# Row and column maxima of an attention and soft-MoE kernel: from a TensorE product to VectorE copies between partition quadrants

## The chip, the cores and the metric

The kernel runs on one core of a Trainium2 chip. The metric is device time in microseconds (us) of one launch. A core has engines that run side by side, each with its own queue of instructions: TensorE (PE in the profile, with PEld for its weight loads), VectorE (DVE), ScalarE (ACT), GpSimd (POOL) and SyncE (SP, which here only issues DMAs). Data lie in SBUF, with 128 partitions, and in the smaller PSUM, into which TensorE writes. A quadrant is a set of 32 neighbouring partitions. VectorE works along the columns of each partition; it can transpose blocks of 32 x 32 but its reductions don't cross the quadrants.

## The reference

First an attention in which keys and values are the same: 16 neighbouring pixels of kv are averaged and multiplied by w_sr. Then a soft mixture of experts over all tokens, whose dispatch is a softmax over the tokens (down each column) and whose combination is a softmax over the slots (along each row).

```python
kv_pool = kv.reshape(B, H // r, r, W // r, r, C).mean(axis=(2, 4))
k = v = kv_pool.reshape(B, -1, C) @ w_sr
s = scale * (q @ k.transpose(0, 2, 1))
s = s - s.max(-1, keepdims=True)
a = np.exp(s)
a /= a.sum(-1, keepdims=True) + 1e-09
x = (a @ v).reshape(B * N, C)

logits = x @ phi
d = np.exp(logits - logits.max(0, keepdims=True))
d /= d.sum(0, keepdims=True) + 1e-09
slot_input = (d.T @ x).reshape(E, S_per_e, D)
for e in range(E):
    slot_out[e] = np.maximum(slot_input[e] @ w1[e], 0.0) @ w2[e]
c = np.exp(logits - logits.max(1, keepdims=True))
c /= c.sum(1, keepdims=True) + 1e-09
out = c @ slot_out
```

Here B = 4 batches of 12288 queries with C = 128 channels meet 768 keys each; there are 8 experts with 4 slots each, so 32 columns in the logits.

## The kernel before

The 49152 queries are cut into 96 blocks of 512. For each block, `qk` makes the scores with the keys on the partitions: six tiles of 128 keys x 512 queries, two to a PSUM tile (`s0`, `s1`, `s2`), each from three products because queries and keys are split in a high and a low part. The softmax needs for each query the maximum over all 768 keys, which lie on partitions and in tiles. That is the row-maximum chain:

- `rowmax1` (L480, three times a block): VectorE transposes blocks of 32 x 32 on the fly and takes the maximum over the 32 keys of each quadrant. What is left has 96 columns: six tiles of keys, 16 groups of 32 queries.
- `rowmax2` (L490, L492): a maximum over the six tiles, then a product with `quad`, which puts each quadrant's 16 numbers in columns of its own, with zeros elsewhere.
- `rowmax_pe` (L500): a TensorE product with `sel`, a matrix of ones where two partitions have the same number within their quadrant. It brings the four quadrants' numbers, side by side, to every partition.
- `rowmax3` (L505): the maximum over the four.
- `rowmax4` (L510): VectorE transposes back and spreads, so that each partition has the maximum of every query (`mb`).

Then `sub` (L518, four pieces) subtracts it from the scores, which frees the three PSUM tiles for the next block. `exp_hi` (L525) and `exp_t` (L529) take the exponential on ScalarE, `plo` (L534) makes the low part on GpSimd, and `av_hi` and `av_lo` (L551, L552, L559) multiply with the values on TensorE, some two blocks later. `av_evac` (L569) brings the result to SBUF.

Four blocks make a group (`group_ops`) for the first half of the mixture: a softmax over the tokens with a running column maximum. `g2` (L628, L630) takes the maximum over the group's tokens in each quadrant. `g2q` spreads it with `quad` on ScalarE, `g3m` (L639) multiplies it with `sel` on TensorE, and `g3` (L644 to L651) takes the maximum over the quadrants, transposes it and updates the running maximum `MRUN`. `g4` to `g7a` use it. After the last block comes a tail with the experts and the combination.

Two PSUM banks, the ring `m`, serve all products but the scores: attention outputs, sums of the groups, keys and values of the next batch, and the products with `sel`. The product of the row maxima uses the top columns of a bank and may lie beside an attention output.

The order of instructions on PE, DVE, ACT and POOL isn't left to a scheduler: `Plan` simulates the engines with a cost for each operation and a due time made of `PER`, the planned time of a block, and writes each engine's queue in the order that results. An operation marked `hot`, as the row-maximum chain is, is kept free of others that would delay it (`HOLD`). `raw` is the wait that the plan reckons between two dependent operations of one engine.

## Time and profile before

| | |
|---|---|
| median of 3 runs | 1114.38 us (1112.85 to 1114.99) |
| profiled execution: its time, its span | 1114.22 us, 1112.4 us |
| mean granted clock of TensorE | 0.975 |
| busy over the span: PE, DVE, ACT, POOL | 1046.7, 984.9, 822.7, 866.2 us |
| first and last row-maximum product (L492 to L500) | 30.1 and 1003.3 us |

The span runs from the first to the last instruction; some 2 us of the time lie around it. Up to about 25 us the first keys are loaded and pooled, from there to about 1010 us the blocks follow one another, and the rest is the tail, with the output's DMAs.

A row of a group names line, engine, operation, output and inputs, shapes and count; then busy time in us and the mean length of one in ns; then the engine's idle time before these instructions and what ended it. A row of the timeline has start, length, engine and line. Shares of several engines don't add up to anything, as they run side by side.

### The profile page before, as it was taken

How to read it: one execution, taken by the hardware profiler on the slowest of the kernel's cores; microseconds unless marked ns; L12 is line 12 of the kernel's file. 1: busy time of each engine (PE TensorE's matmuls, PEld its weight loads, DVE VectorE, ACT ScalarE, POOL GpSimd, SP SyncE). 2: the span in 40 equal slices, each digit the busy share in tenths (PEclk: the TensorE clock that was granted, in tenths of full speed). 3: DMA queues.
4: the chain of work that ended last, by engine and by line, in shares of the span. 5: the costliest groups of instructions: out<-in, count | busy, mean ns of one | idle time of the engine just before them, and what ended most of it. 6: DMA issues, size and time to landing. Idle time of an engine off the chain costs nothing.

```text
span 1112.4 us, 24632 instructions
## 1 busy us (share of the span) xinstructions
PE 1046.7 (94%) x10198; PEld 897.3 (81%) x10198; DVE 984.9 (89%) x1492; ACT 822.7 (74%) x1006; POOL 866.2 (78%) x480
## 2 busy tenths in 40 slices
PE   3699999999999999999999999999999999997876
PEld 2588888888888888888888888888888888886343
DVE  7899889889889989899899988989989988987895
ACT  1677778778778778878877788688788777875563
POOL 0579897788899888789889889779889889773340
PEclk9799999999999999999999999999999999999885
DMA  9315421111125310120136210120110110113398
GB/s 342 117 22 132 96 44 39 39 58 39 39 54 124 91 42 22 39 70 27 39 83 123 71 53 1 39 96 2 39 39 1 39 39 2 39 39 115 141 407 360
DMA packets 17407, 89.15 MB, mean 80 GB/s; under 512 B 1680, under 2 KB 3984, under 8 KB 11152
## 3 DMA queue, kind: packets, MB, share of 16 engines
q1 hardware_dynamic: 13408, 69.47, 16.8%
q0 software_dynamic: 3312, 17.70, 8.4%
q8 instruction: 81, 1.33, 0.5%
q10 hardware_dynamic: 576, 0.41, 0.1%
q14 instruction: 30, 0.25, 0.1%
HBM read 58.87 MB, written 25.17 MB: 76 GB/s over the span
## 4 chain that ended last, share of the span: by engine, by line
PE 67%; DVE 27%; issue 2%; ACT 2%; POOL 1%; DMA 1%; SPq 0%; DVEq 0%; ACTq 0%; POOLq 0%
PE m L551 11%; PE m L552 10%; PE m L559 10%; PE s L473 9%; PE s L475 9%; PE s L474 9%; DVE t L518 8%; DVE r L480 8%; PE m L500 3%; PE m L690 2%; DVE mb L510 2%; PE po L1120 2%; DVE o L1129 2%; DVE cm L628 1%; DVE pool L311 1%
## 5 line engine op out<-in xcount | busy, mean ns | idle before, releaser
L534 POOL TENSOR_TENSOR plo<-t,phi 128x1536 f16<-128x1536 f32 x190 | 595.8, 3143 | 125.1 <-ACT t L529 123.8
L525 ACT ACTIVATE phi<-t,lnk 128x1536 f16<-128x1536 f32 x192 | 301.6, 1571 | 133.5 <-DVE t L518 132.9
L480 DVE TRANSPOSE_TENSOR_REDUCE r<-s 128x32 f32<-128x1024 f32 x288 | 349.8, 1236 | 27.1 <-PE s L475 21.1
L551 PE MATMUL m<-vhi,phi 128*128 128x161 f16 x2280 | 354.5, 234 | 2.5 <-DVE m L505 1.3
L552 PE MATMUL m<-vlo,phi 128*128 128x160 f16 x2280 | 353.5, 233 | 0.0
L518 DVE TENSOR_TENSOR t<-s,mb 128x1024 f32<-128x1024 f32 (+1 forms) x384 | 342.9, 949 | 8.8 <-DVE mb L510 0.9
L529 ACT ACTIVATE t<-t,lnk 128x1536 f32<-128x1536 f32 x192 | 299.8, 1568 | 2.3
L551 PEld LDWEIGHTS <-phi 128*128 128x128 f16 x2304 | 227.0, 99 | 22.9 <-issue 22.8
L473 PE MATMUL s<-qhi,khi 128*128 128x512 f32 x576 | 238.1, 413 | 6.5 <-DVE t L518 6.1
L552 PEld LDWEIGHTS <-phi 128*128 128x128 f16 x2304 | 225.5, 98 | 5.2 <-issue 3.3
L475 PE MATMUL s<-qhi,klo 128*128 128x512 f32 x576 | 227.2, 394 | 0.0
L474 PE MATMUL s<-qlo,khi 128*128 128x512 f32 x576 | 226.6, 393 | 0.0
L559 PE MATMUL m<-vhi,plo 128*128 128x161 f16 x2280 | 221.9, 233 | 0.3 <-POOL plo L534 0.3
L559 PEld LDWEIGHTS <-plo 128*128 128x128 f16 x2304 | 174.8, 100 | 1.3 <-issue 0.6
L463 POOL TENSOR_TENSOR qlo<-q,qhi 128x512 fp32r<-128x512 f32 x96 | 125.7, 1310 | 26.9 <-ACT qhi L459 26.9
L569 ACT ACTIVATE xl<-m 128x322 f32<-128x322 f32 x189 | 81.0, 428 | 76.1 <-PE m L559 75.7
L473 PEld LDWEIGHTS s<-qhi,khi 128*128 128x128 f32 x576 | 109.7, 190 | 29.9 <-issue 3.6
L475 PEld LDWEIGHTS s<-qhi,klo 128*128 128x128 f32 x576 | 109.2, 190 | 24.6 <-DVE klo L353 0.5
L474 PEld LDWEIGHTS s<-qlo,khi 128*128 128x128 f32 x576 | 109.8, 191 | 20.3 <-issue 0.7
L510 DVE STREAM_TRANSPOSE mb<-m 128x512 f32<-128x512 f32 x96 | 68.3, 711 | 3.3
L459 ACT ACTIVATE qhi<-q 128x512 fp32r<-128x512 f32 x96 | 59.2, 617 | 2.4 <-issue 1.0
L505 DVE TENSOR_REDUCE m<-m 128x16 f32<-128x64 f32 x96 | 21.5, 224 | 40.5 <-PE m L500 40.5
(140 smaller groups left out, 854.1 us busy)
## 6 DMA issues: line engine op xcount, KB each, us to landing
q<-qT SPq DMA_DIRECT2D x23, 1024.0 KB, 4.8
outT<-o SPq DMA_DIRECT2D x21, 1024.0 KB, 5.2
kva<-kvT POOLq DMA_DIRECT2D x9, 1536.0 KB, 11.4
kva<-kvT SPq DMA_DIRECT2D x3, 1536.0 KB, 10.5
kv<-kv SPq DMA_DIRECT2D x8, 512.0 KB, 5.7
w<-w SPq DMA_DIRECT2D x2, 1536.0 KB, 6.4
w<-w SPq DMA_DIRECT2D x4, 768.0 KB, 4.6
outT<-o SPq DMA_DIRECT2D x6, 512.0 KB, 4.3
```

What stands on the lines that cost most here:

```text
L463: nc.gpsimd.tensor_tensor(out=lo, in0=q_src(i), in1=hi.bitcast(F32), op=ALU.subtract)
L473: nc.tensor.matmul(s, khi[:, ks], hi, start=True, stop=False)
L474: nc.tensor.matmul(s, khi[:, ks], lo, start=False, stop=False)
L475: nc.tensor.matmul(s, klo[:, ks], hi, start=False, stop=True)
L480: nc.vector.tensor_reduce(out=MX[i][:, 2 * u : 2 * u + 2, :].rearrange("p t b -> p (t b)"), in_=S[i, u].rearrange("p t (b j) -> p (t b) j" ...
L518: nc.vector.tensor_tensor(out=TT_[i, h][:, o : o + n, :], in0=S[i, t // 2][:, u : u + n, :], in1=MX[i].unsqueeze(1).broadcast_to([P, n, BQ ...
L525: nc.scalar.activation(hi, TT_[i, h], AF.Exp, bias=lnk, scale=SCALE)
L529: nc.scalar.activation(t, t, AF.Exp, bias=lnk, scale=SCALE)
L534: eng.tensor_tensor(out=lo, in0=TT_.pop((i, h)), in1=PP[i, h], op=ALU.subtract)
L551: nc.tensor.matmul(px, p, vhi[:, t, :], start=(t == 0), stop=False)
L552: nc.tensor.matmul(px[:, 1:], p, vlo[:, t, :], start=False, stop=False)
L559: nc.tensor.matmul(px, PP[i, t // TH][1][:, t % TH, ks], vhi[:, t, :], start=False, stop=(t == NT - 1))
```

## The change

Row maxima and column maxima no longer go through TensorE. In `rowmax2` the maximum over the tiles is written to the first 16 columns of `rq`, in SBUF; three VectorE copies bring the numbers of quadrants 1, 2 and 3 to columns of their own in quadrant 0. In `rowmax3` four VectorE reductions, all reading quadrant 0, write the maximum over the quadrants to one quadrant each. `rowmax_pe` is gone. The groups do the same in `g2` and `g3`, with one column in place of 16; `g2q` and `g3m` are gone, and the running maximum is now a reduction over a pair of neighbouring columns' blocks, the old maximum and the group's.

The PSUM banks are no longer used for any of this. The plan's numbers change with it: a block is planned at 9.5 us, the new operations have costs of their own, and some costs of TensorE's products are lower, so that the order of the queues can differ from before in other places too. The pair that holds the high and the low part of the exponentials is made earlier; what is computed there is the same.

```diff
-    PER = 9.8
+    PER = 9.5
...
     def rowmax2(i):
-        top = banks[plan.bank][:, 512 - (NQD + 1) * NBK :]
-        pq = PQ[i] = top[:, NBK:]
-        r1 = top[:, :NBK]
-        nc.vector.tensor_reduce(out=r1, in_=MX[i].rearrange("p t b -> p b t"), axis=X, op=ALU.max)
         rq = sp.tile([P, NQD, NBK], F32, tag="rq", name=f"rq_{i}")
-        nc.vector.tensor_tensor(
-            out=rq, in0=r1.unsqueeze(1).broadcast_to([P, NQD, NBK]),
-            in1=quad.unsqueeze(2).broadcast_to([P, NQD, NBK]), op=ALU.mult,
-        )
+        nc.vector.tensor_reduce(out=rq[:, 0, :], in_=MX[i].rearrange("p t b -> p b t"), axis=X, op=ALU.max)
+        for k in range(1, NQD):
+            nc.vector.tensor_copy(rq[:Q32, k, :], rq[k * Q32 : (k + 1) * Q32, 0, :])
         MX[i] = rq
-
-    def rowmax_pe(i):
-        pqv = PQ.pop(i)
-        nc.tensor.matmul(pqv, sel, MX[i].rearrange("p k b -> p (k b)"), start=True, stop=True)
-        MX[i] = pqv
 
     def rowmax3(i):
         m1 = sp.tile([P, NBK], F32, tag="m1", name=f"m1_{i}")
-        nc.vector.tensor_reduce(out=m1, in_=MX[i].rearrange("p (k b) -> p b k", k=NQD), axis=X, op=ALU.max)
+        for k in range(NQD):
+            nc.vector.tensor_reduce(
+                out=m1[k * Q32 : (k + 1) * Q32, :], in_=MX[i][:Q32].rearrange("p k b -> p b k"), axis=X, op=ALU.max
+            )
         MX[i] = m1
...
-        d["cmt"] = sm2(g, "cmt", [P, 1])
-        nc.vector.tensor_reduce(out=d["cmt"], in_=cm, axis=X, op=ALU.max)
-
-    def g2q(g):
-        d = G[g]
         d["cq"] = sm2(g, "cq", [P, NQD])
-        scale(g, d["cq"], quad, d["cmt"])
-
-    def g3m(g):
-        pc = G[g]["pc"] = mt([P, 512], f"pc_{g}")
-        nc.tensor.matmul(pc[:, :NQD], sel, G[g]["cq"], start=True, stop=True)
+        nc.vector.tensor_reduce(out=d["cq"][:, :1], in_=cm, axis=X, op=ALU.max)
 
     def g3(g):
         d = G[g]
+        cq = d["cq"]
+        for k in range(1, NQD):
+            nc.vector.tensor_copy(cq[:Q32, k : k + 1], cq[k * Q32 : (k + 1) * Q32, :1])
         c1 = sm2(g, "c1", [P, 1])
-        nc.vector.tensor_reduce(out=c1, in_=d["pc"][:, :NQD], axis=X, op=ALU.max)
-        d["gm"] = d["pc"][:, NS : 2 * NS]
-        nc.vector.transpose(out=d["gm"], in_=c1.broadcast_to([P, NS]))
-        MRUN[g] = gp.tile([P, NS], F32, tag="mrun", name=f"mrun_{g}", bufs=3)
+        for k in range(NQD):
+            nc.vector.tensor_reduce(out=c1[k * Q32 : (k + 1) * Q32, :], in_=cq[:Q32], axis=X, op=ALU.max)
+        MR[g + 1] = gp.tile([P, 2, NS], F32, tag="mrun", name=f"mrun_{g}", bufs=3)
+        new = MRUN[g] = MR[g + 1][:, 0, :]
         if g == 0:
-            nc.vector.tensor_copy(MRUN[g], d["gm"])
+            nc.vector.transpose(out=new, in_=c1.broadcast_to([P, NS]))
         else:
-            nc.vector.tensor_tensor(out=MRUN[g], in0=MRUN[g - 1], in1=d["gm"], op=ALU.max)
+            nc.vector.transpose(out=MR[g][:, 1, :], in_=c1.broadcast_to([P, NS]))
+            nc.vector.tensor_reduce(out=new, in_=MR[g].rearrange("p k n -> p n k"), axis=X, op=ALU.max)
...
-        go("2q", small, sm_(1), [o["2"]], g2q)
-        mc, md = ("m", ("pc", g)), ("m", ("pd", g))
-        go("3m", "PE", 0.25, [o["2q"]], g3m, acq=[mc])
-        go("3", "DVE", 0.45, [o["3m"]] + ([ops["g3", g - 1]] if g else []), g3, use=[mc])
+        go("3", "DVE", 1.3, [o["2"]] + ([ops["g3", g - 1]] if g else []), g3)
...
-                "PE", 3 * 0.2315, 0.17, T0 - QKP + 0.65 * t, [ops["ql", i]] + kd[: 1 if t < KSPLIT // P else 2] + ([ops["qk", i, t - 1]] if t else [ops["qk", i - 1, NT - 1]] if i else []),
+                "PE", 3 * 0.2275, 0.17, T0 - QKP + 0.65 * t, [ops["ql", i]] + kd[: 1 if t < KSPLIT // P else 2] + ([ops["qk", i, t - 1]] if t else [ops["qk", i - 1, NT - 1]] if i else []),
...
-        r2 = op("DVE", 0.36, 0.08, T0 + 2, [ops["r", i, NU - 1]], lambda i=i: rowmax2(i), acq=[("m", ("pq", i)), ("rq", i)], use=[("r6", i)], hot=True, raw=0.14)
-        pe = op("PE", 0.27, 0.3, T0 - 10, [r2], lambda i=i: rowmax_pe(i), use=[("m", ("pq", i)), ("rq", i)], hot=True)
-        r3 = op("DVE", 0.12, 0.08, T0 - 10, [pe], lambda i=i: rowmax3(i), acq=[("m1", i)], use=[("m", ("pq", i))], hot=True)
-        r4 = op("DVE", dve(BQ) - 0.03, 0.08, T0 - 10, [r3], lambda i=i: rowmax4(i), acq=[("mb", i)], use=[("m1", i)], hot=True, raw=0.14)
+        r2 = op("DVE", 0.46, 0.08, T0 + 2, [ops["r", i, NU - 1]], lambda i=i: rowmax2(i), acq=[("rq", i)], use=[("r6", i)], hot=True, raw=0.1)
+        r3 = op("DVE", 0.4, 0.08, T0 - 10, [r2], lambda i=i: rowmax3(i), acq=[("m1", i)], use=[("rq", i)], hot=True, raw=0.18)
+        r4 = op("DVE", dve(BQ) + 0.03, 0.08, T0 - 10, [r3], lambda i=i: rowmax4(i), acq=[("mb", i)], use=[("m1", i)], hot=True, raw=0.18)
```

The costs of the AV products in the plan go from 0.0705 to 0.0695 (`av_hi`) and from 0.072 to 0.070 (`av_lo`) for each matmul.

## The prediction

> **What bounds the kernel now.** I read the busy times first, then the steady stretch from 100 to 1000 us, then what VectorE waits for there.

> ```profile
> 100.00:1000.00 900.00, 889.53 (x8898) 783.85 (x8897) 815.05 (x1202) 706.72 (x841) 776.89 (x415) 1.00 0.18 49
> ```

> The columns are length, then busy time of PE, weight loads, DVE, ACT and POOL, the granted clock, the DMA share and GB/s. TensorE is busy 889.5 of 900 us at full clock, so it sets the pace; VectorE follows with 815.1. The groups of VectorE in the same stretch show how near it is:

> ```profile
> L480 DVE TRANSPOSE_TENSOR_REDUCE r<-s 128x32 f32<-128x1024 f32 x264 | 320.1, 1235 | 24.2 <-PE s L475 18.7
> L518 DVE TENSOR_TENSOR t<-s,mb 128x1024 f32<-128x1024 f32 x176 | 214.4, 1218 | 8.1 <-DVE mb L510 0.9
> L510 DVE STREAM_TRANSPOSE mb<-m 128x512 f32<-128x512 f32 x88 | 62.6, 711 | 3.0
> L490 DVE TENSOR_REDUCE m<-r 128x16 f32<-128x96 f32 x88 | 28.8, 328 | 5.3
> L492 DVE TENSOR_TENSOR rq<-m,quad 128x64 f32<-128x64 f32 x88 | 19.7, 224 | 3.0
> L505 DVE TENSOR_REDUCE m<-m 128x16 f32<-128x64 f32 x88 | 19.7, 223 | 35.8 <-PE m L500 35.8
> L696 DVE TENSOR_TENSOR acc<-acc,m 128x129 f32<-128x129 f32 x22 | 6.2, 282 | 2.2 <-ACT acc L585 2.2
> ```

> The stretch holds 88 blocks (x88), so one block takes 900 / 88 = 10.23 us. Of VectorE's 900 - 815 = 85 us idle, 35.8 is the wait for the matmul of the row maxima, 18.7 the wait for scores and 2.2 a wait for ScalarE. The other 28.2 us are short gaps before dependent instructions, which I count as not to be filled. One block of VectorE is thus 815 / 88 + 28.2 / 88 = 9.26 + 0.32 = 9.58 us of work and 0.65 us of waits. Both engines stand close to the limit, and the change takes work from one and gives work to the other.

> **What goes.**

> ```profile
> L500 PE MATMUL m<-rq,sel 128*128 128x64 f32 x176 | 36.7, 290 | 8.1 <-DVE rq L492 7.5
> L639 PE MATMUL m<-cq,sel 128*128 128x4 f32 x46 | 6.7, 216 | 0.0
> ```

> TensorE loses 36.7 + 6.7 us of work and 8.1 us of idle time in the stretch. Its floor falls from 889.5 / 88 = 10.11 to (889.5 - 43.4) / 88 = 9.61 us a block. Were TensorE still the bound, 0.5 us x 96 blocks = 48 us would go (1066 us). That is the far low end. What is late next is VectorE.

> ScalarE loses a scaling per group, worth nothing here, as it is busy 706.7 of 900. The two PSUM banks lose two tenants, the product of the row maxima and that of the column maxima. No row shows a large wait for a bank, so I give that nothing. No DMA moves, and SP's and POOL's queues issue the same instructions as before. The new waits are all of VectorE on itself, in the row-maximum chain; what stands behind them is the transpose L510 and the four subtractions L518, which ScalarE's exponentials and the next scores wait for, so nothing covers them.

> VectorE's fixed part is what stays when the chain from L490 to L510 is cut out. From busy time and gaps it loses L490, L492, L505 and the gap before L492: 815.1 + 28.2 - 28.8 - 19.7 - 19.7 - 3.0 = 772.1 us, or 8.77 us a block. The gaps before L490 and L510 stay in this number.

> **What the new chain costs.** It is a reduction of 96 columns, three copies of 32 x 16, and four reductions of 32 x 64 to 32 x 16, one for each quadrant. The trace has no instruction on 32 partitions, so I take the same shapes on 128.

> ```profile
> 1027.48 0.26 DVE L1025 COPY sm<-m 128x16 f32<-128x16 f32 x2
> L1025 DVE COPY sm<-m 128x16 f32<-128x16 f32 x2 | 0.3, 170 | 0.1
> 439.61 0.32 DVE L490 TENSOR_REDUCE m<-r 128x16 f32<-128x96 f32 x1
> 439.97 0.22 DVE L492 TENSOR_TENSOR rq<-m,quad 128x64 f32<-128x64 f32 x1
> 440.78 0.22 DVE L505 TENSOR_REDUCE m<-m 128x16 f32<-128x64 f32 x1 [0.50 <-PE m L500]
> 441.04 0.71 DVE L510 STREAM_TRANSPOSE mb<-m 128x512 f32<-128x512 f32 x1
> ```

> Two independent copies of 16 columns take 0.17 us each and 0.26 us together: the second starts 0.09 us after the first, an overlap of 0.08 us. A dependent instruction starts 0.03 to 0.04 us after the end of the one before (440.78 + 0.22 to 441.04). So:

> - reduction, as L490: 0.33, and 0.03 to the copies
> - three copies, pitch 0.09: 2 x 0.09 + 0.17 = 0.35, and 0.03
> - four reductions as L505, pitch 0.22 - 0.08 = 0.14: 3 x 0.14 + 0.22 = 0.64

> The sum is 1.38 us. Before, the same stretch was 1.43 us from start to start (439.61 to 441.04), 0.50 of it a wait. Seen so, the change shortens the chain's latency a little, but it turns a wait into work, and the wait could hold other work.

> The durations are uncertain both ways. L505 reads PSUM in strides; the new reductions read SBUF in strides, as L238 below did: 128 columns in 0.36 us, against 0.28 for L244, which reads the same columns in order.

> ```profile
> 9.27 0.36 DVE L238 TENSOR_REDUCE sel<-ident 128x32 f32<-128x128 f32 x1
> 9.55 0.28 DVE L244 TENSOR_REDUCE quad<-ident 128x4 f32<-128x128 f32 x1
> 9.74 0.22 DVE L240 COPY sel<-sel 128x128 f32<-128x128 f32 x1
> ```

> That 0.08 us on 128 columns would be 0.04 to 0.05 on 64, in each of four: up to 0.2 more. Downward, a reduction that writes SBUF could be 0.08 shorter than L490, which writes PSUM, and copies could follow each other at 0.06: together 0.16 less. I take 1.38, by the rows of the same shapes.

> **The groups.** Before the running maximum there were L644, L646 and L651; now there are three copies of one column, four reductions of four columns, the same transpose, and a reduction of pairs.

> ```profile
> 1018.35 0.16 DVE L644 TENSOR_REDUCE c<-m 128x1 f32<-128x4 f32 x1 [0.81 <-PE m L639]
> 1018.55 0.23 DVE L646 STREAM_TRANSPOSE m<-c 128x32 f32<-128x32 f32 x1
> 1018.81 0.19 DVE L651 TENSOR_TENSOR mrun<-mrun,m 128x32 f32<-128x32 f32 x1
> ```

> Added: copies 0.35 + 0.03, reductions 3 x 0.08 + 0.16 + 0.03 = 0.43, pairs 0.22 + 0.03. That is 1.06 us. Gone: 0.16 + 0.19 + 0.03 = 0.38. So 0.68 us for each group of four blocks, 0.17 a block; bounds 0.1 and 0.3.

> **The sum.** VectorE's block is 8.77 + 1.38 + 0.17 = 10.32 us, against 10.23 now. TensorE's 9.61 is out of the way. The difference is 0.09 us x 96 blocks = 9 us. The profiled execution took 1114.2 us (span 1112.4), 0.2 under the median of the three runs, so the forecast is **1123 us**. The own range of this case: with the 0.16 taken off, 10.16 us and 1107; with 0.2 for the strides and 0.2 for waits on scores that stay (18.7 / 88), 10.73 us and 1162.

> **Rivals.**

> *Faster: the small operations cost less than their lookalikes.* The chain and the group together pay as long as 8.77 + chain + 0.17 stays under 10.23, so the point from which it turns is a chain of 1.29 us, only 0.09 under my sum. With 0.25 for the first reduction, copies 0.06 apart (0.27 together), and reductions 0.09 apart with 0.20 for the last (0.47), it is 1.05 with its two gaps, the block 9.99, and the gain 0.24 x 96 = 23 us: 1091. For it speaks that TensorE then leaves more than 0.3 us of slack; against it that no row has such a pitch for 64 columns. Chance 0.31.

> *Slower: the small operations don't overlap.* Each copy reads another quadrant, and each reduction writes another; in the trace before all neighbours start on the same partitions, so the overlap of 0.08 us is not shown for these. Without it, five neighbours in the chain (two copies, three reductions) cost 0.08 to 0.11 more each, 0.40 to 0.55, and five in a group a quarter of that per block. The block is 10.82 to 11.01 us, and the time 1171 to 1189, about 1180. Chance 0.22. [...]

> *Slower by much: the copies wait for GpSimd.* L240 copied 128 columns within SBUF in 0.22 us, where L244 needed 0.28 to reduce as many, so such a copy seems to use more of the memory's paths. And the trace shows VectorE stopped by GpSimd:

> ```profile
> 7.94 1.22 DVE L311 TENSOR_TENSOR pool<-pool,kv 128x1024 f32<-128x1024 f32 x1 [0.39 <-DMA kv<-kv]
> L311 DVE TENSOR_TENSOR pool<-pool,kv x12: 681/956/2165, 7.9 to 23.4; 128x1024 f32<-128x1024 f32 x6, 128x512 f32<-128x512 f32 x6
> 10.67 1.54 POOL L463 TENSOR_TENSOR qlo<-q,qhi 128x512 fp32r<-128x512 f32 x1 [9.14 <-ACT qhi L459]
> L534 POOL TENSOR_TENSOR plo<-t,phi 128x1536 f16<-128x1536 f32 x176 | 551.2, 3139 | 105.0 <-ACT t L529 103.7 <-DVE cm L628 0.8
> L463 POOL TENSOR_TENSOR qlo<-q,qhi 128x512 fp32r<-128x512 f32 x87 | 113.5, 1305 | 0.0
> ```

> One addition of two SBUF tiles took 2.17 us in place of 1.22; the only GpSimd work of that stretch, 10.67 to 12.21, lies beside it. If a copy also waits for GpSimd's running instruction, the mean rest of one met at random is (2 x 3.14^2 + 1.31^2) / (2 x 10.23) = 1.05 us. With one such wait a block the time is 10.32 + 1.05 = 11.37 us a block: 1114 + 1.14 x 96 = 1224 us; with more, far above. Against it: copies are not additions of two tiles, and reductions (L701, L490) show no such rests. Chance 0.12. [...]

> **How the numbers follow.** Forecast 0.35, faster rival 0.31, no overlap 0.22, GpSimd 0.12. About 0.2% (2 us) can be told from no change. Of the forecast's 0.35, some 0.05 lies below that band, 0.09 in it and 0.21 above. So faster is 0.31 + 0.05 = 0.36, same 0.09, slower 0.21 + 0.22 + 0.12 = 0.55. The range for 8 in 10 runs from 1090, the faster rival's time, to 1190, the end of the second; it leaves out the third and the tail below.

> **What would show it.** TensorE busy near 9.6 us a block with idle time before the scores or the AV matmuls, released by VectorE; VectorE busy about 95% or more from 100 to 1000 us, without the 35.8 us wait. The four reductions should start 0.14 us apart, the copies 0.09. Starts 0.2 us or more apart show the second rival; copies of a microsecond, while GpSimd is in an instruction, the third. A chain under 1.29 us from the first reduction to the transpose, with the score waits of 18.7 us gone, proves the forecast's sign wrong.

## The result and the profile after

The changed kernel takes 1570.95 us (median of 4 runs, 1567.14 to 1571.80) against 1114.68 before: a ratio of 1.4097, with a 95% interval of 1.4076 to 1.4118. The profiled execution has a span of 1568.7 us.

First the page of the changed kernel: the busy times, the granted clock in 40 slices, and the first lines of the chain that ended last.

```profile
span 1568.7 us, 24659 instructions
PE 1171.9 (75%) x9956; PEld 978.7 (62%) x9956; DVE 1401.6 (89%) x2120; ACT 840.3 (54%) x982; POOL 865.6 (55%) x480
PEclk8888888888788798887888888888887888888886
DVE 62%; PE 33%; issue 4%; ACT 1%; DMA 0%; POOL 0%; DVEq 0%; SPq 0%; ACTq 0%
DVE rq L490 21%; DVE r L480 11%; DVE t L511 11%; PE s L473 10%; PE s L474 9%; PE s L475 8%; DVE m L496 6%; DVE mb L503 4%; DVE rq L488 2%; PE po L1106 2%; PE m L679 1%; DVE o L1115 1%; DVE cm L622 1%; DVE c L633 1%; DVE pool L311 1%
```

VectorE's busy time grew from 984.9 to 1401.6 us, by 417 of the 456 us. One line leads the chain: L490, the copies between the quadrants. TensorE has less work than before (9956 products in place of 10198) and a longer busy time (1171.9 us in place of 1046.7), and the third row shows what goes with it: up to the last slice its granted clock is 0.7 to 0.9 of full speed, 0.85 in the mean, where the mean was 0.975.

Now VectorE's groups of the whole span, and one of TensorE's, in the columns of before.

```profile
L480 DVE TRANSPOSE_TENSOR_REDUCE r<-s 128x32 f32<-128x1024 f32 x288 | 355.0, 1242 | 95.3 <-PE s L475 90.2
L490 DVE COPY rq<-rq 32x16 f32<-32x16 f32 x288 | 333.4, 1158 | 5.9
L496 DVE TENSOR_REDUCE m<-rq 32x16 f32<-32x64 f32 x384 | 95.9, 250 | 7.2
L488 DVE TENSOR_REDUCE rq<-r 128x16 f32<-128x96 f32 x96 | 30.8, 321 | 3.3
L473 PE MATMUL s<-qhi,khi 128*128 128x512 f32 x576 | 305.4, 530 | 343.4 <-DVE t L511 343.4
```

A copy of 32 x 16 takes 1158 ns in the mean. That is no length of work: the view of line L490 gives the shortest, the median and the longest, and below it stands the same view for the groups' copies of a single column.

```profile
L490 DVE COPY rq<-rq x288: 161/438/3117, 29.9 to 1459.2; 32x16 f32<-32x16 f32 x144
L630 DVE COPY cq<-cq x75: 141/142/145, 127.7 to 1478.5; 32x1 f32<-32x1 f32 x75
```

161 ns is what the copy needs; the rest, up to 2956 ns, is waiting, inside the instruction, where no semaphore and so no releaser shows it. The longest is about as long as one GpSimd subtraction (3.11 us below). The timelines of one block, first VectorE's, then GpSimd's, show it instruction by instruction.

```profile
410.07 3.55 DVE L511 TENSOR_TENSOR t<-s,mb 128x1024 f32<-128x1024 f32 x4
...
418.74 0.32 DVE L488 TENSOR_REDUCE rq<-r 128x16 f32<-128x96 f32 x1
419.09 0.34 DVE L490 COPY rq<-rq 32x16 f32<-32x16 f32 x1
419.45 3.05 DVE L490 COPY rq<-rq 32x16 f32<-32x16 f32 x1
422.51 1.21 DVE L490 COPY rq<-rq 32x16 f32<-32x16 f32 x1
423.76 1.03 DVE L496 TENSOR_REDUCE m<-rq 32x16 f32<-32x64 f32 x4
425.64 3.55 DVE L511 TENSOR_TENSOR t<-s,mb 128x1024 f32<-128x1024 f32 x4
```

```profile
415.26 3.13 POOL L528 TENSOR_TENSOR plo<-t,phi 128x1536 f16<-128x1536 f32 x1 [7.14 <-DVE r L480]
418.35 1.06 POOL L617 TENSOR_TENSOR LL<-xl,ru 128x512 f32<-128x512 f32 x1
419.37 3.11 POOL L528 TENSOR_TENSOR plo<-t,phi 128x1536 f16<-128x1536 f32 x1
422.44 1.26 POOL L463 TENSOR_TENSOR qlo<-q,qhi 128x512 fp32r<-128x512 f32 x1
```

The first copy ends at 419.43, when GpSimd's L617 ends (419.41). The second ends at 422.50; GpSimd's next instruction ends at 422.48. The third ends at 423.72, and `qlo` at 423.70. Between one copy and the next, GpSimd's next instruction gets in, and the next copy waits for its end. The same holds over the whole trace: of the 288 copies 182 take more than 0.19 us, and every one of these ends 0.02 to 0.04 us after the end of a GpSimd instruction (179 times a tensor operation, 3 times a memset).

### The profile page after: what moved, and what is told of

It reads as the page before. It is cut to its first block, busy times and chain, and to the rows that moved or that the text cites. A ratio compares the mean times of both kernels' runs of the same rounds, so it can differ in the third digit from the quotient of the medians.

```text
span 1568.7 us, 24659 instructions
## 1 busy us (share of the span) xinstructions
PE 1171.9 (75%) x9956; PEld 978.7 (62%) x9956; DVE 1401.6 (89%) x2120; ACT 840.3 (54%) x982; POOL 865.6 (55%) x480
## 2 busy tenths in 40 slices
DMA packets 17409, 89.15 MB, mean 57 GB/s; under 512 B 1680, under 2 KB 3984, under 8 KB 11152
## 3 DMA queue, kind: packets, MB, share of 16 engines
q8 instruction: 79, 1.29, 0.3%
## 4 chain that ended last, share of the span: by engine, by line
DVE 62%; PE 33%; issue 4%; ACT 1%; DMA 0%; POOL 0%; DVEq 0%; SPq 0%; ACTq 0%
DVE rq L490 21%; DVE r L480 11%; DVE t L511 11%; PE s L473 10%; PE s L474 9%; PE s L475 8%; DVE m L496 6%; DVE mb L503 4%; DVE rq L488 2%; PE po L1106 2%; PE m L679 1%; DVE o L1115 1%; DVE cm L622 1%; DVE c L633 1%; DVE pool L311 1%
## 5 line engine op out<-in xcount | busy, mean ns | idle before, releaser
L473 PE MATMUL s<-qhi,khi 128*128 128x512 f32 x576 | 305.4, 530 | 343.4 <-DVE t L511 343.4
L480 DVE TRANSPOSE_TENSOR_REDUCE r<-s 128x32 f32<-128x1024 f32 x288 | 355.0, 1242 | 95.3 <-PE s L475 90.2
L473 PEld LDWEIGHTS s<-qhi,khi 128*128 128x128 f32 x576 | 147.4, 256 | 397.5 <-issue 347.5
L490 DVE COPY rq<-rq 32x16 f32<-32x16 f32 x288 | 333.4, 1158 | 5.9
L474 PE MATMUL s<-qlo,khi 128*128 128x512 f32 x576 | 286.7, 498 | 0.0
L475 PE MATMUL s<-qhi,klo 128*128 128x512 f32 x576 | 280.3, 487 | 0.0
L545 PEld LDWEIGHTS <-phi 128*128 128x128 f16 x2304 | 225.3, 98 | 25.0 <-issue 23.4
L475 PEld LDWEIGHTS s<-qhi,klo 128*128 128x128 f32 x576 | 145.8, 253 | 39.3 <-DVE klo L353 0.4
L474 PEld LDWEIGHTS s<-qlo,khi 128*128 128x128 f32 x576 | 148.4, 258 | 31.2
L463 POOL TENSOR_TENSOR qlo<-q,qhi 128x512 fp32r<-128x512 f32 x96 | 122.7, 1279 | 48.3 <-ACT qhi L459 47.8
L459 ACT ACTIVATE qhi<-q 128x512 fp32r<-128x512 f32 x96 | 59.9, 625 | 79.5 <-PE s L475 77.7
L496 DVE TENSOR_REDUCE m<-rq 32x16 f32<-32x64 f32 x384 | 95.9, 250 | 7.2
```

The source lines that it names most:

```text
L473: nc.tensor.matmul(s, khi[:, ks], hi, start=True, stop=False)
L474: nc.tensor.matmul(s, khi[:, ks], lo, start=False, stop=False)
L475: nc.tensor.matmul(s, klo[:, ks], hi, start=False, stop=True)
L480: nc.vector.tensor_reduce(out=MX[i][:, 2 * u : 2 * u + 2, :].rearrange("p t b -> p (t b)"), in_=S[i, u].rearrange("p t (b j) -> p (t b) j" ...
L490: nc.vector.tensor_copy(rq[:Q32, k, :], rq[k * Q32 : (k + 1) * Q32, 0, :])
L545: nc.tensor.matmul(px, p, vhi[:, t, :], start=(t == 0), stop=False)
```

## The experiments

### Copies made by reductions

```diff
-            nc.vector.tensor_copy(rq[:Q32, k, :], rq[k * Q32 : (k + 1) * Q32, 0, :])
+            nc.vector.tensor_reduce(
+                out=rq[:Q32, k, :], in_=rq[k * Q32 : (k + 1) * Q32, 0, :].unsqueeze(2), axis=X, op=ALU.max
+            )
```

> The three copies of the row maxima are made by reductions over an axis of length one; everything else is the changed kernel. Theory A (a copy within SBUF waits for GpSimd's running instruction, a reduction does not): each of the three takes about 0.17 us in place of 1.16, the chain is 0.33 + 0.04 + 0.52 + 0.03 + 1.04 = 1.96 us, the block 8.77 + 1.96 + 0.25 (groups) = 10.98 us plus 0 to 0.2 of waits for scores, the time 1114 + 0.75 to 0.95 x 96 = 1186 to 1205 us. Theory B (any VectorE instruction that reads another quadrant is slow): it stays near 1571 us.

It took 1209.79 us, a ratio of 1.0863 (1.0845 to 1.0881) to before. Line L490 of this kernel, in the same view as above:

```profile
L490 DVE TENSOR_REDUCE rq<-rq x288: 156/157/161, 30.3 to 1097.0; 32x16 f32<-32x16 f32 x144
```

The same bytes go the same way between the same quadrants in 156 to 161 ns, every time, although GpSimd is busy 746.7 of the 950 us from 100 to 1050. B falls, and the order of the queues, which is that of the changed kernel, isn't the cause either: 361 of the 456 us are the wait of the copies and what hangs on it. The time is 5 us above A's range. The group of the first maxima in this run has 31.2 us of waits for scores, 0.33 a block, where up to 0.2 was reckoned:

```profile
L480 DVE TRANSPOSE_TENSOR_REDUCE r<-s 128x32 f32<-128x1024 f32 x288 | 346.7, 1229 | 32.1 <-PE s L475 31.2
```

### Copies out of PSUM

```diff
-        nc.vector.tensor_reduce(out=rq[:, 0, :], in_=MX[i].rearrange("p t b -> p b t"), axis=X, op=ALU.max)
-        for k in range(1, NQD):
-            nc.vector.tensor_copy(rq[:Q32, k, :], rq[k * Q32 : (k + 1) * Q32, 0, :])
+        r1 = banks[plan.bank][:, 512 - NBK :]
+        nc.vector.tensor_reduce(out=r1, in_=MX[i].rearrange("p t b -> p b t"), axis=X, op=ALU.max)
+        for k in range(NQD):
+            nc.vector.tensor_copy(rq[:Q32, k, :], r1[k * Q32 : (k + 1) * Q32, :])
```

In the plan the row maxima then hold a place in the ring `m` again.

> The changed kernel, but the first reduction of the row maxima writes to PSUM, and four copies (one more than before) bring it to the quadrant 0 columns. Theory A, in the form that only copies within SBUF wait: a copy takes 0.17 us, the chain is 0.33 + 0.04 + 0.68 + 0.03 + 1.04 = 2.12 us, and the time is 1114 + 0.91 to 1.1 x 96 = 1200 to 1220 us. If every copy that writes SBUF waits, it is near 1571 us or, with a fourth copy, above.

1235.18 us, a ratio of 1.1086 (1.1064 to 1.1108): 15 us above the range, but far from 1571. The waits for scores are 33.9 us here, 0.35 a block, where up to 0.19 was reckoned; that is about the 15. The group of the copies:

```profile
L491 DVE COPY rq<-m 32x16 f32<-32x16 f32 x384 | 64.6, 168 | 7.1
```

168 ns in the mean of 384, where the copies within SBUF took 1158: the same operation with its source in PSUM does not wait. So it is not copies as such, but copies of this size whose source and result both lie in SBUF.

### The maximum of a tile with itself

```diff
-            nc.vector.tensor_copy(rq[:Q32, k, :], rq[k * Q32 : (k + 1) * Q32, 0, :])
+            q = rq[k * Q32 : (k + 1) * Q32, 0, :]
+            nc.vector.tensor_tensor(out=rq[:Q32, k, :], in0=q, in1=q, op=ALU.max)
```

> The changed kernel, with each of the three copies made as the maximum of the source with itself, an operation with two SBUF inputs. If the wait comes with what takes GpSimd's way to SBUF, two inputs as well as a copy (as the addition of 2.17 us did in the trace of before), the time stays near 1571 us and the operations take about 1.1 us; if it is a matter of copies alone, 0.16 us each and 1210 us.

1575.77 us, and the group looks like that of the copies:

```profile
L491 DVE TENSOR_TENSOR rq<-rq 32x16 f32<-32x16 f32 x288 | 336.1, 1167 | 5.9
```

This operation with two SBUF inputs waits as the copy within SBUF does; a reduction of one SBUF input does not: 1167 and 1158 ns in the mean against 158. Why these two wait and the reduction does not, no run shows.

### GpSimd's subtraction in thirds

```diff
-        eng.tensor_tensor(out=lo, in0=TT_.pop((i, h)), in1=PP[i, h][0], op=ALU.subtract)
+        t = TT_.pop((i, h))
+        for c in range(TH):
+            eng.tensor_tensor(out=lo[:, c, :], in0=t[:, c, :], in1=PP[i, h][0][:, c, :], op=ALU.subtract)
```

> The changed kernel, with GpSimd's subtraction for the low part cut into three instructions of 512 columns; VectorE's instructions are untouched. Theory A (a copy waits until GpSimd's running instruction ends): what a copy waits falls from 0.99 us to roughly 0.4, as GpSimd's instructions become about 1.05 to 1.3 us long in place of 3.1; the longest copy falls from 3.1 to below 1.6 us; the time is 1380 to 1430 us. Theory B (copies between quadrants are slow by themselves): copies and time stay, 1571 us or a little more.

1459.72 us, 30 us above A's range, with VectorE's instructions untouched. Line L490 and GpSimd's group:

```profile
L490 DVE COPY rq<-rq x288: 161/1103/1223, 30.1 to 1351.4; 32x16 f32<-32x16 f32 x144
L530 POOL TENSOR_TENSOR plo<-t,phi 128x512 f16<-128x512 f32 x570 | 645.2, 1160 | 416.1 <-ACT t L523 406.1 <-DVE r L602 5.0 <-DVE r L480 4.9
```

The longest copy fell from 3117 to 1223 ns, as A has it. The mean wait did not fall to 0.4 us: the mean copy takes 878 ns in place of 1158, and the median rose from 438 to 1103 ns, close to one whole GpSimd instruction of 1160. I had taken the copies to meet GpSimd at random. They don't: they queue up behind it. The next run asks how.

### The exponential twice

```diff
-        nc.scalar.activation(hi, TT_[i, h], AF.Exp, bias=lnk, scale=SCALE)
+        for _ in range(2 - h):
+            nc.scalar.activation(hi, TT_[i, h], AF.Exp, bias=lnk, scale=SCALE)
```

> The changed kernel, with one more run of the first exponential for the first half of each block (1.57 us of ScalarE, the result unchanged); ScalarE is busy 54% of the span. Theory E (the copies tie a block's row maxima to GpSimd's work on the block before, so that subtraction, exponentials, GpSimd's subtractions and copies make one loop): the delay goes through the loop, 1.5 us x 96 = 144 us, 1680 to 1725 us. Theory F (the copies meet GpSimd's instructions at random and wait a mean rest): ScalarE has room for it, 1571 us within 15.

1701.61 us, 131 us more than the changed kernel, in E's range, on an engine that is busy half the time. What went in is 96 exponentials of 1.57 us, 151 us.

```profile
L490 DVE COPY rq<-rq 32x16 f32<-32x16 f32 x288 | 427.0, 1483 | 5.9
L480 DVE TRANSPOSE_TENSOR_REDUCE r<-s 128x32 f32<-128x1024 f32 x288 | 358.0, 1246 | 118.7 <-PE s L475 113.8
```

The copies grew by 93.6 us (333.4 to 427.0) and the waits for scores by 23.6; before the subtractions VectorE sits idle no longer than in the changed kernel (5.4 us), so most of the delay reaches them through the copies. F falls; the same exponentials in the kernel with reductions, where no copy waits, were not tried. The block is a loop: the subtraction of block i (from 410.07), its exponentials on ScalarE, GpSimd's work on its low parts (from 415.26 to 423.70, with what stands between), the copies of block i + 1, which wait for that, and the subtraction of block i + 1 (425.64): 15.57 us around. Before the change, no step of the row maxima waited for GpSimd: the longest L490 took 338 ns and the longest L492 225 ns, with medians of 328 and 224.

### The attention's products thrice

```diff
+        for r in range(2):
+            for t in range(NT):
+                nc.tensor.matmul(px, PP[i, t // TH][0][:, t % TH, ks], vhi[:, t, :], start=(t == 0), stop=(t == NT - 1))
```

(at the head of `av_hi`)

> The changed kernel, with the attention's products of the high parts made two more times (12 matmuls more for each 128 queries, the result unchanged), so that TensorE idles less: some 3.4 us more work in a block of 15 us, of which 3.5 us are idle now. Theory C (the lower granted clock, 0.86 in place of 1.00, comes from TensorE's idle time and makes scores late): the granted clock rises towards 1.0, the score products fall from 0.50 to near 0.40 us, VectorE's waits for scores shrink from 90 us, and the time falls by 20 to 60 us although there is more work. Rival: the clock is no matter of idle time, and the added work delays scores; the time rises by 20 us or more.

1601.11 us, 30 us more, so the rival's sign, and not the fall of 20 to 60 us that C forecast. But the clock did as C says: in the stretch from 100 to 1450 us it is 0.97, where the changed kernel has 0.86 (first row: the changed kernel; second: this one).

```profile
100.00:1450.00 1350.00, 1030.86 (x8863) 878.78 (x8862) 1222.63 (x1815) 739.69 (x838) 793.56 (x423) 0.86 0.13 35
```

```profile
100.00:1450.00 1350.00, 1202.94 (x12954) 1082.47 (x12953) 1270.22 (x1778) 727.83 (x824) 780.80 (x419) 0.97 0.13 35
```

And VectorE's groups of this kernel:

```profile
L490 DVE COPY rq<-rq 32x16 f32<-32x16 f32 x288 | 417.3, 1449 | 5.9
L480 DVE TRANSPOSE_TENSOR_REDUCE r<-s 128x32 f32<-128x1024 f32 x288 | 349.2, 1234 | 43.8 <-PE s L475 41.8
```

The waits for scores fell from 90.2 to 41.8 us, and the copies grew from 333.4 to 417.3: 48 us less and 84 us more, near the 30 us of the time. That VectorE waits at the copies for what it gained before them follows from the loop; why it lost more than it gained was not tried. The first score product of a tile fell with the clock from 530 to 442 ns in the mean (L473). So the lower clock goes with TensorE's idle time: 319 of the 1350 us idle at 0.86, 147 at 0.97. What it costs by itself isn't shown, as it was lifted by added work.

### Each part alone

The row maxima as in the changed kernel with the groups as before, then the groups alone in the kernel before. The edits put back, or take over, `g2` to `g3` and their lines in `group_ops`; this is the plan's part of the first:

```diff
-        go("3", "DVE", 1.3, [o["2"]] + ([ops["g3", g - 1]] if g else []), g3)
+        go("2q", small, sm_(1), [o["2"]], g2q)
+        mc, md = ("m", ("pc", g)), ("m", ("pd", g))
+        go("3m", "PE", 0.25, [o["2q"]], g3m, acq=[mc])
+        go("3", "DVE", 0.45, [o["3m"]] + ([ops["g3", g - 1]] if g else []), g3, use=[mc])
```

> The changed kernel with the groups' column maxima as before (TensorE, ScalarE): the row maxima's part alone. By the sum VectorE loses 0.25 us a block: 1571 - 23 = 1548 us. If what is freed is taken up by the copies' waits, as it was with the added products: 1560 to 1575 us. Either way the row maxima make nearly all of the 456 us.

1569.04 us: 2 us less than the changed kernel, no more than its own runs differ by. Taking VectorE's group work away gives nothing, because the waits take up what is freed:

```profile
L480 DVE TRANSPOSE_TENSOR_REDUCE r<-s 128x32 f32<-128x1024 f32 x288 | 357.7, 1245 | 114.3 <-PE s L475 105.6
L490 DVE COPY rq<-rq 32x16 f32<-32x16 f32 x288 | 342.9, 1191 | 5.9
```

The copies grew by 9.5 us and the waits for scores by 15.4.

> The kernel before, with the groups' column maxima alone moved to VectorE (copies of one column, small reductions); the row maxima stay with TensorE, and so do the plan's numbers. In the changed kernel this stretch takes 1.62 us a group where it took 0.64, so VectorE gets 0.98 / 4 = 0.25 us a block more, and TensorE loses 0.08. Theory: VectorE's 9.58 us of work a block become 9.83, still under the block's 10.23, most of it taken from its waits: 1108 to 1125 us. Rival: VectorE's work adds in full, 0.25 x 96 = 23 us: 1138 us.

1134.06 us, a ratio of 1.0188 (1.0172 to 1.0203): 20 us of the rival's 23. My theory, that VectorE's waits would take most of it, was wrong. The stretch from 100 to 1000 us of this run, and the wait for the row maxima in it:

```profile
100.00:1000.00 900.00, 868.08 (x8663) 756.97 (x8661) 820.04 (x1302) 690.90 (x803) 760.87 (x410) 1.00 0.17 47
```

```profile
L506 DVE TENSOR_REDUCE m<-m 128x16 f32<-128x64 f32 x86 | 19.2, 224 | 36.1 <-PE m L501 36.1
```

TensorE has gone from 889.5 to 868.1 us busy (86 blocks in place of 88), and the wait for the row maxima, 36.1 us for 86 blocks, is what it was (35.8 for 88): the added work didn't fill it. So VectorE's waits in the kernel before were no room for this work, and TensorE didn't set the pace alone. How much of the 20 us comes from another order of the queues was not tried; the next run shows what order alone can cost.

### The planning numbers alone

```diff
-    PER = 9.8
+    PER = 9.5
...
-                "PE", 3 * 0.2315, 0.17, ...
+                "PE", 3 * 0.2275, 0.17, ...
```

(and the two costs of `av_hi` and `av_lo`)

> The kernel before with the changed kernel's planning numbers (a block of 9.5 us, the lower costs of TensorE's products) and nothing else, so that only the order in the queues can differ. Theory: the order is worth little, 1108 to 1122 us. Rival: the new order has a part in the slowdown, 1125 us or more.

1121.60 us, a ratio of 1.0073 (1.0057 to 1.0090): in the kernel before, the other order costs 8 us, in the theory's range.

### Small instructions that stay in their quadrants

Against the kernel with copies made by reductions:

```diff
-            nc.vector.tensor_reduce(
-                out=rq[:Q32, k, :], in_=rq[k * Q32 : (k + 1) * Q32, 0, :].unsqueeze(2), axis=X, op=ALU.max
-            )
+            nc.vector.tensor_reduce(out=rq[:, k, :], in_=rq[:, 0, :].unsqueeze(2), axis=X, op=ALU.max)
...
-        m1 = sp.tile([P, NBK], F32, tag="m1", name=f"m1_{i}")
+        m4 = sp.tile([P, NQD, NBK], F32, tag="m1", name=f"m1_{i}", bufs=1)
+        m1 = m4[:, 0, :]
...
-            nc.vector.tensor_reduce(
-                out=m1[k * Q32 : (k + 1) * Q32, :], in_=MX[i][:Q32].rearrange("p k b -> p b k"), axis=X, op=ALU.max
-            )
+            nc.vector.tensor_reduce(out=m4[:, k, :], in_=MX[i].rearrange("p k b -> p b k"), axis=X, op=ALU.max)
```

> The kernel with reductions in place of copies, but the three and the four small reductions work on all 128 partitions and write columns of their own, so that no input or output starts in another quadrant; the maximum is then that of each quadrant alone. Count and columns are the same. Theory D (crossing to another quadrant takes the overlap away): the three start 0.09 us apart in place of 0.17, the four 0.17 apart in place of 0.26, 0.17 + 0.27 = 0.44 us a block less: 1210 - 42 = 1168 us. Rival (small instructions never overlap): the starts and the time stay, 1210 us.

1134.87 us, a ratio of 1.0191 (1.0173 to 1.0210), 75 us under the reductions that cross, and 33 under the 1168 that D gave. The timelines of VectorE, first of the crossing kernel (copies made by reductions), then of this one:

```profile
408.88 0.32 DVE L488 TENSOR_REDUCE rq<-r 128x16 f32<-128x96 f32 x1
409.24 0.51 DVE L490 TENSOR_REDUCE rq<-rq 32x16 f32<-32x16 f32 x3
409.78 1.05 DVE L498 TENSOR_REDUCE m<-rq 32x16 f32<-32x64 f32 x4
410.87 0.71 DVE L505 STREAM_TRANSPOSE mb<-m 128x512 f32<-128x512 f32 x1
```

```profile
414.17 0.32 DVE L488 TENSOR_REDUCE rq<-r 128x16 f32<-128x96 f32 x1
414.52 0.32 DVE L490 TENSOR_REDUCE rq<-rq 128x16 f32<-128x16 f32 x3
414.88 0.78 DVE L497 TENSOR_REDUCE m<-rq 128x16 f32<-128x64 f32 x4
415.57 0.70 DVE L502 STREAM_TRANSPOSE mb<-m 128x512 f32<-128x512 f32 x1
```

Three of 0.16 us take 0.51 us where they cross and 0.32 where they don't; four of 0.25 take 1.05 and 0.78. The starts move as D says, for both steps: 0.19 + 0.27 = 0.46 us x 96 = 44 of the 75 us. From the first reduction to the transpose it is 1.99 against 1.40 us; the other 0.13 us (12 us in all) come from the transpose, which here needs only the first of the four and so starts before the last has ended. Waits for scores make 13 us more, 31.2 to 18.0; the last 6 us are open:

```profile
L480 DVE TRANSPOSE_TENSOR_REDUCE r<-s 128x32 f32<-128x1024 f32 x288 | 346.3, 1228 | 19.2 <-PE s L475 18.0
```

In these rows each small instruction behind the first starts 0.09 to 0.10 us later where it crosses (0.51 - 0.32 over two, 1.05 - 0.78 over three). One thing stays untested: the edit also takes these operations from 32 to 128 partitions, and no run has operations on 32 partitions that stay in their quadrants, so whether the crossing or the number of partitions takes the overlap away is not shown.

### One maximum, then spread

Against the kernel with copies made by reductions:

```diff
-        for k in range(NQD):
-            nc.vector.tensor_reduce(
-                out=m1[k * Q32 : (k + 1) * Q32, :], in_=MX[i][:Q32].rearrange("p k b -> p b k"), axis=X, op=ALU.max
-            )
+        nc.vector.tensor_reduce(out=m1[:Q32, :], in_=MX[i][:Q32].rearrange("p k b -> p b k"), axis=X, op=ALU.max)
+        for k in range(1, NQD):
+            nc.vector.tensor_reduce(out=m1[k * Q32 : (k + 1) * Q32, :], in_=m1[:Q32, :].unsqueeze(2), axis=X, op=ALU.max)
```

> The kernel with reductions in place of copies; the maximum over the quadrants is taken once, in quadrant 0, and brought to the other three by reductions over an axis of length one. 1.05 us become 0.25 + 0.03 + 3 x 0.16 = 0.76 us: 0.28 us a block less, 1210 - 27 = 1183 us if VectorE's work counts in full; still slower than the kernel before.

1174.82 us, a ratio of 1.0550 (1.0531 to 1.0569), 35 us less than with four maxima, where 27 were reckoned. It is the fastest of the kernels that do the whole crossing on VectorE, and 5.5% slower than the one before. No version that beats the kernel before came out of these runs.

## Why the prediction was wrong

- **Forecast: 1123 us, measured 1571.** Slower came true, but not by the forecast's sum. The sum was that of a kernel in which the small operations neither wait for GpSimd nor lose their overlap. Such a kernel was run: with quadrants kept and reductions in place of copies it takes 1134.87 us, some 12 of them saved by its early transpose. The chain of 1.38 us measures 0.71 + 0.78 = 1.49 there (414.17 to 414.88, and the four reductions), as the reductions of 64 columns take 0.25 us and not L505's 0.22. The fixed part of 8.77 us comes out there as about 8.6 (86 blocks in 900 us, 10.47, less 1.40 for the chain, 0.25 for the groups and 0.19 of score waits). "What is late next is VectorE" holds there too: it is busy 857.6 of 900 us, TensorE 845.7.
- **The step that failed** is "I take the same shapes on 128": the price of the copies came from L1025, whose copies read PSUM, while the change copies within SBUF. L1025's 170 ns is right for copies out of PSUM (168 in `copies_from_psum`) and says nothing of the others, which took 1158 ns. The prediction held the evidence (an addition of two SBUF tiles that took 2.17 us beside a GpSimd instruction, and L240's copy, which at 0.22 us was faster than a reduction at 0.28) and gave the case 0.12.
- **The size of that rival** was wrong too. It priced one wait a block at the mean rest of a GpSimd instruction, 1.05 us, and gave 1224 us. The copies took 333.4 / 96 = 3.47 us a block, because GpSimd's next instruction can get in before each of the three, and because the waits close a loop: with 1.57 us of exponentials added the block grew by 131 / 96 = 1.36 us. A mean over random meetings doesn't describe two engines that wait for each other in turn.
- **The second rival, no overlap,** was right in the starts that it forecast and was taken as an alternative to the third. Both came together: from the 1135 us without either, the missing overlap, the later transpose and more waits for scores lead to 1210, and the copies' waits to 1571.
- **The groups:** 0.68 us a group was mis-sized, as the small operations there don't overlap either (three copies of 0.14 us in 0.46 us, four reductions of 0.15 in 0.63); from the copies to the running maximum it is 1.62 us where it was 0.64, so 0.98, 0.25 us a block and not 0.17. In the kernel before, this part alone costs 20 us; in the changed kernel it costs no more than runs differ by, since the loop sets the time.
- **The lower bounds** were too low. No row showed the 0.08 us off the first reduction or the copies 0.06 apart; they were guesses. A first reduction that writes SBUF takes 0.32 us (L488), hardly under L490's 0.33, and copies 0.06 apart come to 0.27 us only at 0.15 each, where the sum has 0.17.
- **TensorE's floor of 9.61 us** had no bearing, but "full clock" did not last: with TensorE waiting for the subtractions 343 us in all, its granted clock fell from 0.975 to 0.85 in the mean.
- **What was to show it** did: copies of a microsecond while GpSimd is in an instruction (third rival), and starts 0.26 us apart in the four reductions (second).

## What to carry to other kernels

Before a small VectorE operation is moved into a stretch where GpSimd is busy, look at where its operands lie: with source and result in SBUF a copy of 16 columns, or a maximum with two SBUF inputs, stood here for up to a whole GpSimd instruction (the longest took 3.12 and 3.11 us, a GpSimd subtraction 3.11), several times over, and the profile shows it as a long instruction and not as a wait. A reduction over an axis of length one (158 ns) or a source in PSUM (168 ns) made the same move without waiting. And take the price of an operation from a row with the same memories, the same partitions and the same starting quadrants, not only the same columns.

## What the runs showed of the hardware that was not expected

The three copies of a block can wait for a GpSimd instruction each, even when all three are ready at once: between two copies 0.02 us apart GpSimd's next instruction gets in (419.43, 419.45, 422.50 above). All three wait (over 0.19 us) in 29 of the 96 blocks, two in 43, one in 9, none in 15. A copy of one column never waited: 141 to 145 ns in all 75, of which 66 lie wholly within a GpSimd subtraction. Why one column differs from 16 is not shown.

In the stretch below TensorE's granted clock follows its idle time within microseconds, 2.7 to 6.0. The windows of 5 us of the changed kernel, TensorE alone (length, busy time, granted clock, DMA share, GB/s):

```profile
395.00:400.00 5.00, 4.35 (x10) 0.50 0.00 0
400.00:405.00 5.00, 5.00 (x43) 0.83 0.01 3
405.00:410.00 5.00, 2.86 (x41) 1.00 0.62 210
410.00:415.00 5.00, 3.55 (x9) 0.69 0.00 0
415.00:420.00 5.00, 5.00 (x50) 0.97 0.00 0
```

Subtractions begin at 410.07 and at 425.64, and TensorE waits for the first piece to free a tile (it is idle for 3.59 us before 411.45). The chain of waits shows score products after the first of these at 0.43 us each, and a faster one 3 us later:

```profile
412.24 0.43 PE s L475
412.67 0.43 PE s L473
...
415.23 0.33 PE s L473
```

Cut into finer windows, this trace has the clock at half (0.50) from 394.8 to 401.7 and from 411.9 to 415.3: it falls 2.7 and 4.0 us after TensorE's last product has ended, the second time 0.5 us after the next has begun, and is full again 6.0 and 3.9 us after the next begins. Score products start 0.43 us apart while it is at half and 0.22 to 0.24 us apart once it is full. These are two falls and two rises of one trace; what sets their delays is not shown.
